# DMA transposes for q and the spatial weights, natural token order and a new order of units in an attention and gated-MLP kernel

## The chip, the cores and the metric

One core of a Trainium2 chip runs the whole program. The metric is device time in microseconds (us). *Slow* is a run more than 1.5% above the fastest of the same kernel; only fast runs are compared. Ratios are the mean time of one kernel's fast runs over the mean of the other's fast runs of the same rounds on the same chip, so not quite the ratio of the medians quoted beside them. A profile's span is about 1.8 us shorter than the time of the same run.

## The reference, cut to what matters

Four batches, eight heads, 768 tokens, head size 64. Each head's keys and values are mixed over 8 blocks of 96 tokens by a Sinkhorn-normalised 8x8 matrix P; attention runs inside each block; its output, 512 wide, goes through an MLP whose gate mixes tokens with a 768x768 matrix.

```python
k_sorted = np.einsum('bhij,bhjcd->bhicd', P, k_b)          # v the same
attn = softmax(scale * q_b @ k_sb^T)                       # inside a block of 96
x = (attn @ v_sb), heads side by side                      # 4 x 768 x 512
h = np.maximum(x @ w_in, 0.0); u, v = halves of h          # 512 wide each
v_n = (v - mean) / sqrt(var + 1e-6)
v_s = np.einsum('ts,bsd->btd', w_spatial, v_n) + b_spatial[None, :, None]
out = (u * v_s) @ w_out
```

## The kernel before

TensorE (PE), VectorE (DVE), ScalarE (ACT) and GpSimd (POOL) run a fixed list of units in program order, each written as letter, number, batch, copying engine and PSUM slot: `v`, `k` mix values and keys, `q` transposes q, `s` scores, `a` attend, `d` divide, `V`, `U` projections, `N` normalisation, `S` spatial product, `O` output projection. Batch b's MLP is interleaved with batch b+1's attention. There are four PSUM slots. In the tables and traces, xt is the divided attention output, lns the log-sum and then its exponential, vs the spatial sum, gt the gate product.

```python
# q: 48 transposes of 128x64 per batch on PE, two copies out of PSUM
nc.tensor.transpose(t[hh*64:hh*64+64, x, g*128:(g+1)*128],
                    q_in[self.b][:, 2*hp+hh, g*D:(g+1)*D], ident_bf)
copy(eng, qT, t[:, :, 0:S])
# spatial weights: 36 transposes of 128x128 on PE, six copies
nc.tensor.transpose(tp[:, 0, go*128:(go+1)*128],
                    wsp_nat[:, go, :].rearrange("p (s g) -> p g s", g=G)[:, gs, :], ident_bf)
# division: tokens stay in the order (g, block, t)
nc.scalar.activation(out=lns, in_=t[:, 1, 0:HW], func=AF.Ln)
nc.scalar.activation(out=lns, in_=lns, func=AF.Exp, scale=-1.0)
nc.vector.tensor_mul(
    out=self.xt[hp].rearrange("p (g i t) -> p i g t", g=G, i=NB)[:, i0:i0+NB//2],
    in0=t[:, 0, 0:HW].rearrange("p (i g t) -> p i g t", g=G, t=TB),
    in1=lns.rearrange("p (i g t) -> p i g t", g=G, t=TB))
# loads of batch b+2, issued by POOL before the first gate product of batch b
if not gmlp[b].gt and b + 2 < B:
    ... gate = two copies out of vb of batch b+1      # waits until vb has landed
    v_in[b+2], q_in[b+2], k_in[b+2] = load_heads(...), load_heads(...), load_heads(...)
    # [cut]
```

Loads are issued by POOL; stores, the trip of the mixed values through DRAM (`vd`, `vb`) and, in the changed kernel, the transposes are issued by the sync engine in order.

The softmax here doesn't subtract the row's maximum and nothing guards it: scores larger than these inputs give would overflow.

## Time and profile before

| | before |
|---|---|
| time, median of fast runs | 166.2 us |
| first projection (V00) starts, in the profile | 28.96 us |
| V00 to V01, V01 to V02, V02 to V03 | 37.9, 37.8, 33.7 us |
| V03 to the end | 29.4 us |

The rows below "first projection" are read from PE's timeline: V01 is the start of the first projection of batch 1, and so on; V00 is counted from where its matmuls run on (one single matmul of it stands earlier, at 28.13 us). The profile of before is of a slow run (169.51 us), so its stage times are up to 3.3 us long in sum.

### The profile page before, as it was taken

The numbers are of one execution on the slowest core, as the hardware profiler recorded it, in microseconds if no ns is written. First come the engines' busy times: TensorE is split into PE (matmuls) and PEld (weight loads), VectorE is DVE, ScalarE is ACT, GpSimd is POOL, SyncE is SP. The second block draws the span as 40 slices with busy tenths as digits, with TensorE's granted clock in tenths as the row PEclk, the third lists the DMA queues.
The fourth block names the chain that finished last, engine by engine and source line by source line (L and its number), as shares of the span: only waits on it lengthen the run. The fifth ranks groups of instructions, "written<-read, shape, count | busy, mean of one in ns | idle before, by whom it ended". The sixth has DMA issues, their size and how long they took to land.

```text
span 167.7 us, 3907 instructions
## 1 busy us (share of the span) xinstructions
PE 151.9 (91%) x1636; PEld 88.6 (53%) x1645; DVE 97.4 (58%) x203; ACT 110.0 (66%) x181; POOL 43.1 (26%) x46
## 2 busy tenths in 40 slices
PE   0989986999999999999994999999999999999780
PEld 0266853556855544457662454457665544556330
DVE  4667887158971562389222265789232658849951
ACT  3167997459877777689954586489959974560041
POOL 7931000970029550000049330000063300000000
PEclk9999997599999999999999699999999999999999
DMA  2999999999647997604329993605400036000045
GB/s 15 197 204 209 232 257 187 205 203 236 217 110 96 203 204 193 250 33 151 129 72 160 204 195 131 250 31 178 151 23 0 4 131 250 0 0 4 0 182 193
DMA packets 21554, 23.86 MB, mean 142 GB/s; under 512 B 736, under 2 KB 18144, under 8 KB 21408
## 3 DMA queue, kind: packets, MB, share of 16 engines
q0 software_dynamic: 13760, 12.58, 46.8%
q1 hardware_dynamic: 7776, 11.02, 18.3%
q8 instruction: 13, 0.21, 0.5%
q14 instruction: 5, 0.04, 0.1%
HBM read 27.14 MB, written 8.65 MB: 213 GB/s over the span
## 4 chain that ended last, share of the span: by engine, by line
PE 62%; DVE 11%; ACT 10%; DMA 6%; issue 6%; POOL 2%; DVEq 0%; POOLq 0%; SPq 0%; ACTq 0%
PE ps L393 13%; PE ps L443 13%; PE ps L465 10%; PE ps L428 9%; PE ps L352 4%; ACT ex L338 3%; DVE vs L454 3%; PE ps L331 3%; DMA vb<-vd 3%; PE ps L359 2%; DVE gt L455 2%; PE ps L288 2%; PE ps L246 2%; PE ps L276 2%; PE ps L212 2%
## 5 line engine op out<-in xcount | busy, mean ns | idle before, releaser
L443 PE MATMUL ps<-wspT,v_sb 128*128 128x384 bf16 x192 | 34.6, 334 | 0.0
L338 ACT ACTIVATE ex<-ps 96x768 bf16<-96x768 f32 x32 | 24.3, 806 | 8.4 <-PE ps L331 8.3
L454 DVE TENSOR_TENSOR vs<-ps,b_bc 128x768 f32<-128x768 f32 (+1 forms) x20 | 15.9, 794 | 23.7 <-PE ps L443 18.8
L375 DVE TENSOR_TENSOR xt<-ps,lns 128x384 bf16<-128x384 f32 x32 | 16.9, 554 | 19.9 <-ACT lns L371 19.9
L455 POOL TENSOR_TENSOR gt<-vs,u_sb 128x768 bf16<-128x768 f32 x12 | 19.7, 1651 | 34.1 <-ACT ex L338 31.3
L443 PEld LDWEIGHTS <-v_sb 128*128 128x128 bf16 x192 | 18.2, 100 | 12.6 <-issue 1.6
L393 PE MATMUL ps<-w_in_sb,xt 128*128 128x512 bf16 x94 | 24.1, 406 | 0.3 <-DVE xt L375 0.2
L465 PE MATMUL ps<-w_out_sb,gt 128*128 128x512 bf16 x90 | 21.9, 380 | 1.1 <-DVE gt L455 0.8
L407 DVE BATCH_NORM_STATS2 stats<-v_sb 128x6 f32<-128x512 bf16 x24 | 16.3, 677 | 11.0 <-ACT v_sb L227 10.9
L428 PE MATMUL ps<-xt,w_in_sb 128*128 128x384 bf16 x128 | 22.6, 326 | 0.0
L227 ACT ACTIVATE v_sb<-ps 128x1024 bf16<-128x1024 f32 (+1 forms) x15 | 12.5, 852 | 15.5 <-PE ps L393 15.5
L365 ACT ACTIVATE lns<-ps 128x384 f32<-128x384 f32 x32 | 14.5, 486 | 3.9 <-PE ps L359 3.8
L428 PEld LDWEIGHTS <-w_in_sb 128*128 128x128 bf16 x128 | 12.2, 98 | 8.1
L221 ACT COPY o_sb<-ps 128x256 f32<-128x256 f32 (+1 forms) x11 | 7.3, 663 | 13.8 <-DVE o_sb L223 12.1
L393 PEld LDWEIGHTS <-xt 128*128 128x128 bf16 x96 | 9.9, 104 | 12.1 <-issue 2.1
L371 ACT ACTIVATE lns<-lns 128x384 f32<-128x384 f32 x32 | 15.7, 525 | 0.2
L465 PEld LDWEIGHTS <-gt 128*128 128x128 bf16 x96 | 8.6, 98 | 12.4 <-DVE gt L455 1.3
L352 PE MATMUL ps<-ex,vb 96*64 96x96 bf16 x256 | 11.4, 210 | 3.4 <-DVE vs L454 2.5
L352 PEld LDWEIGHTS <-vb 96*64 96x64 bf16 x256 | 8.7, 109 | 8.5 <-issue 7.1
L227 ACT ACTIVATE u_sb<-ps 128x768 bf16<-128x768 f32 x13 | 10.3, 808 | 1.7 <-PE ps L428 1.2
L359 PE MATMUL ps<-ex,ones 96*64 96x384 bf16 x64 | 11.1, 332 | 0.0
L221 ACT CAST kT<-ps 128x768 bf16<-128x768 f32 x13 | 10.0, 806 | 1.1 <-PE ps L288 1.1
(73 smaller groups left out, 177.8 us busy)
## 6 DMA issues: line engine op xcount, KB each, us to landing
out_dram<-o_sb SPq DMA_DIRECT2D x9, 512.0 KB, 2.8
q_in<-in_q_dram POOLq DMA_DIRECT2D x4, 768.0 KB, 10.4
k_in<-in_k_dram POOLq DMA_DIRECT2D x4, 768.0 KB, 13.4
v_in<-in_v_dram POOLq DMA_DIRECT2D x4, 768.0 KB, 9.7
vd<-vm SPq DMA_DIRECT2D x6, 384.0 KB, 3.7
vb<-vd SPq DMA_DIRECT2D x6, 384.0 KB, 3.9
out_dram<-o_sb SPq DMA_DIRECT2D x6, 256.0 KB, 2.1
wsp_nat<-in_moe_w_spatial_dram POOLq DMA_DIRECT2D x1, 1152.0 KB, 21.9
```

The lines of the kernel that those rows point to most:

```text
L221: nc.scalar.copy(out=out, in_=in_)
L227: nc.scalar.activation(out=out, in_=in_, func=AF.Relu)
L338: nc.scalar.activation(out=e.rearrange("p h i c -> p h (i c)"), in_=t[0:BLK, :, 0:NB // 2 * BLK], func=AF.Exp, scale=scale,)
L352: nc.tensor.matmul(t[hh * 64:hh * 64 + 64, 0, ii * BLK:(ii + 1) * BLK], lhsT=self.vb[:, i, h // (H // 2), h % (H // 2), :], rhs=self.e[n][ ...
L375: nc.vector.tensor_mul(out=self.xt[hp].rearrange("p (g i t) -> p i g t", g=G, i=NB)[:, i0:i0 + NB // 2], in0=t[:, 0, 0:HW].rearrange("p (i ...
L393: nc.tensor.matmul(t[:, x, :], lhsT=self.xt[kc][:, g * 128:(g + 1) * 128], rhs=w_in_sb[:, kc, DH:DFF], start=(kc == 0), stop=(kc == KC - 1),)
L407: nc.vector.bn_stats(out=stats, in_=v_sb[:, x, :])
L428: nc.tensor.matmul(t[:, x, 0:HW], lhsT=w_in_sb[:, kc, mc * 128:(mc + 1) * 128], rhs=self.xt[kc][:, x * HW:(x + 1) * HW], start=(kc == 0), ...
L443: nc.tensor.matmul(t[:, x, 0:HW], lhsT=self.v[g][:, mc * 128:(mc + 1) * 128], rhs=wspT[:, g, x * HW:(x + 1) * HW], start=(g == 0), stop=(g ...
L454: nc.vector.tensor_add(out=vs[:, x], in0=t[:, x, 0:HW], in1=b2[:, x])
L455: eng.tensor_mul(out=gt2[:, x], in0=vs[:, x], in1=u2[:, x])
L465: nc.tensor.matmul(t[:, x, :], lhsT=self.gt[mc][:, g * 128:(g + 1) * 128], rhs=w_out_sb[:, mc, :], start=(mc == 0), stop=(mc == FC - 1),)
```

## The change

Its intent: TensorE is the busy engine, so take the transposes off it. q of batches 1 to 3 and the spatial weights go through transposing DMAs from SBUF to SBUF. For that, tokens must be in natural order, which the division produces by reading at a stride. The spreading of P moves to the start, idle matmuls are put into batch 0's attention to hold the clock, the loads move, and the units are reordered. Cut to its core:

```diff
+        def qdma(self, n, eng, ps):
+            qr = qr_pool.tile([128, G, H, D], BF16, name="qr", tag="qr")
+            nc.vector.tensor_copy(out=qr.rearrange("p g h d -> p h g d"), in_=q_in[self.b]...)
+            nc.sync.dma_start(out=self.q_tile(), in_=qr..., transpose=True)
+    def wsp_t():                       # called before the list of units
+        for g in range(G):
+            nc.sync.dma_start(out=wspT[:, :, g*128:(g+1)*128], in_=wsp_nat[:, g, :], transpose=True)
             # divide
-                out=self.xt[hp].rearrange("p (g i t) -> p i g t", ...)[:, i0:i0 + NB // 2],
-                in1=lns.rearrange("p (i g t) -> p i g t", g=G, t=TB),
+                out=self.xt[hp][:, ih*HW:(ih+1)*HW].rearrange("p (i t g) -> p i t g", ...),
+                in1=lns.rearrange("p (i g t) -> p i t g", g=G, t=TB),
             # first loads, in order
-        w_in, b, w_spatial, v1, k1, q1, w_out
+        w_in, v1, q1, w_spatial, k1, b, w_out
             # loads of batch b+2
-                    if not gmlp[b].gt and b + 2 < B:          # before gate product 1: v, q, k
+                    if len(gmlp[b].gt) == 2:                  # after gate product 2: gate, v
+                    elif len(gmlp[b].gt) == 4:                # after gate product 4: q, k
-                    eng = DVE if b == B - 1 else nc.gpsimd
+                    eng = DVE if b == B - 1 and len(gmlp[b].gt) == FC - 1 else nc.gpsimd
-        vs_pool bufs=2
+        vs_pool bufs=3
 ... [cut: pdiag straight from PSUM, two DVE block transposes of P, four idle matmuls
          in each attend unit of batch 0, natural rows in the store, the new list of units]
```

More of the change, by code (lines that the diff above doesn't have):

```diff
@@ L65 @@
     qk_pool = ctx.enter_context(tc.tile_pool(name="qk", bufs=7))
-    ex_pool = ctx.enter_context(tc.tile_pool(name="ex", bufs=7))
+    qr_pool = ctx.enter_context(tc.tile_pool(name="qr", bufs=1))
+    qt_pool = ctx.enter_context(tc.tile_pool(name="qt", bufs=2))
+    ex_pool = ctx.enter_context(tc.tile_pool(name="ex", bufs=8))
     xt_pool = ctx.enter_context(tc.tile_pool(name="xt", bufs=8))
-    ln_pool = ctx.enter_context(tc.tile_pool(name="ln", bufs=4))
+    ln_pool = ctx.enter_context(tc.tile_pool(name="ln", bufs=3))
     moe_pool = ctx.enter_context(tc.tile_pool(name="moe", bufs=4))
-    vs_pool = ctx.enter_context(tc.tile_pool(name="vs", bufs=2))
+    vs_pool = ctx.enter_context(tc.tile_pool(name="vs", bufs=3))
     vsb_pool = ctx.enter_context(tc.tile_pool(name="vsb", bufs=4))
@@ L88 @@
     nc.sync.dma_start(out=p_all, in_=sort_net.rearrange("b h i j -> (b h) i j"))
-    b_nat = pers.tile([128, S], FP32)
     def load_heads(x, b, name):
@@ L112 @@
     )
-    sel16 = const.tile([8, 128], BF16)
-    nc.gpsimd.memset(sel16, 0.0)
+    sel = const.tile([BH, NB // 2, 128], BF16)
+    nc.gpsimd.memset(sel, 0.0)
     nc.gpsimd.affine_select(
-        out=sel16.rearrange("p (j t) -> p j t", t=TB),
-        in_=sel16.rearrange("p (j t) -> p j t", t=TB),
-        pattern=[[1, NB], [0, TB]], compare_op=ALU.not_equal,
+        out=sel.rearrange("p i (j t) -> p i j t", t=TB),
+        in_=sel.rearrange("p i (j t) -> p i j t", t=TB),
+        pattern=[[NB, NB // 2], [1, NB], [0, TB]], compare_op=ALU.not_equal,
         fill=1.0, base=0, channel_multiplier=-1,
@@ L130 @@
     nc.gpsimd.dma_start(out=w_in_sb, in_=moe_w_in.rearrange("(kc p) f -> p kc f", p=128))
-    nc.gpsimd.dma_start(out=b_nat, in_=_raw_ap(moe_b_spatial, 0, [[0, 128], [1, S]]))
+    v_in[1] = load_heads(v, 1, "v_in")
+    q_in[1] = load_heads(q, 1, "q_in")
     wsp_nat = pers.tile([128, G, S], BF16)
-    nc.gpsimd.dma_start(out=wsp_nat, in_=moe_w_spatial.rearrange("(p g) s -> p g s", g=G))
-    v_in[1] = load_heads(v, 1, "v_in")
+    nc.gpsimd.dma_start(out=wsp_nat, in_=moe_w_spatial.rearrange("(g p) s -> p g s", p=128))
     k_in[1] = load_heads(k, 1, "k_in")
-    q_in[1] = load_heads(q, 1, "q_in")
+    b_bc = pers.tile([128, S], FP32)
+    nc.gpsimd.dma_start(out=b_bc, in_=_raw_ap(moe_b_spatial, 0, [[0, 128], [1, S]]))
     w_out_sb = pers.tile([128, FC, DM], BF16)
@@ L172, with make_pdiag, transpose_p @@
     prep_sb = pers.tile([128, B, NB, H], BF16)
-    pts = {}
-    def spread_t(b, nb, ps):
-        n = nb * NB * H
-        t = ps_tile(ps)
-        for i in range(NB):
-            nc.tensor.matmul(
-                t[0:NB, 0, 0:n].rearrange("p (b i h) -> p b i h", i=NB, h=H)[:, :, i, :],
-                lhsT=p_bf[:, i, :], rhs=ident_bf[0:BH, b * H:(b + nb) * H],
-                start=True, stop=True,
-            )
-        pts[b] = small.tile([NB, B * NB * H], BF16, name="pt", tag="pt", bufs=2)
-        nc.vector.tensor_copy(out=pts[b][:, 0:n], in_=t[0:NB, 0, 0:n])
+    pdiag = [pd_pool.tile([128, H, NB, TB], BF16, name="pdiag") for _ in range(B)]
+    def make_pdiag(b, eng, h0, n, src=None):
+        base = h0 if src is not None else b * NB * H + h0
+        src = prep_sb if src is None else src
+        eng.tensor_mul(
+            out=pdiag[b][:, h0:h0 + n],
+            in0=_raw_ap(mask16, 0, [mask16.ap[0], [0, n], [TB, NB], [1, TB]]),
+            in1=_raw_ap(src, base, [src.ap[0], [1, n], [H, NB], [0, TB]]),
+        )
+    p_t = pers.tile([BH, 2, BH], BF16)
+    def transpose_p():
+        for x in range(2):
+            nc.vector.transpose(
+                out=p_t[:, x, :], in_=p_bf[:, x * (NB // 2):(x + 1) * (NB // 2), :].rearrange("p i j -> p (i j)"),
+            )
     def spread(b, nb, ps):
@@ L191, in spread @@
         t = ps_tile(ps)
-        nc.tensor.matmul(t[:, 0, 0:n], lhsT=sel16, rhs=pts[b][:, 0:n], start=True, stop=True)
-        nc.vector.tensor_copy(
-            out=prep_sb[:, b:b + nb].rearrange("p b i h -> p (b i h)"), in_=t[:, 0, 0:n],
-        )
-    pdiag = [pd_pool.tile([128, H, NB, TB], BF16, name="pdiag") for _ in range(B)]
-    def make_pdiag(b, eng, h0, n):
-        eng.tensor_mul(
-            out=pdiag[b][:, h0:h0 + n],
-            in0=_raw_ap(mask16, 0, [mask16.ap[0], [0, n], [TB, NB], [1, TB]]),
-            in1=_raw_ap(prep_sb, b * NB * H + h0, [prep_sb.ap[0], [1, n], [H, NB], [0, TB]]),
-        )
-    b_bc = pers.tile([128, S], FP32)
-    wspT = pers.tile([128, G, S], BF16)
-    def wsp_unit(gs, eng, ps):
-        tp = ps_tile(ps, BF16)
-        for go in range(G):
-            nc.tensor.transpose(
-                tp[:, 0, go * 128:(go + 1) * 128],
-                wsp_nat[:, go, :].rearrange("p (s g) -> p g s", g=G)[:, gs, :],
-                ident_bf,
+        if b:
+            nc.tensor.matmul(t[:, 1, :], lhsT=ident_bf, rhs=warm_sb, start=True, stop=True)
+        for i in range(NB):
+            nc.tensor.matmul(
+                t[:, 0, 0:n].rearrange("p (b i h) -> p b i h", i=NB, h=H)[:, :, i, :],
+                lhsT=sel[:, i % (NB // 2), :],
+                rhs=p_t[:, i // (NB // 2), b * H:(b + nb) * H],
+                start=True, stop=True,
+            )
+        if b == 0:
+            for h0, nh in ((0, 2), (2, 2), (4, 4)):
+                make_pdiag(0, DVE, h0, nh, t.rearrange("p x c -> p (x c)"))
+        else:
+            nc.vector.tensor_copy(
+                out=prep_sb[:, b:b + nb].rearrange("p b i h -> p (b i h)"), in_=t[:, 0, 0:n],
+            )
+    wspT = pers.tile([128, G, S], BF16)
+    def wsp_t():
+        for g in range(G):
+            nc.sync.dma_start(
+                out=wspT[:, :, g * 128:(g + 1) * 128], in_=wsp_nat[:, g, :], transpose=True,
             )
-        copy(eng, wspT[:, gs, :], tp[:, 0, 0:S])
     def copy(eng, out, in_):
@@ L238, in __init__ @@
             self.vm = None
-            self.q, self.k, self.e, self.vT = {}, {}, {}, {}
+            self.qT, self.q, self.k, self.e, self.vT = None, None, {}, {}, {}
             self.xt, self.vb, self.acc, self.mixed = {}, None, {}, []
@@ L267, in vmix, with q_tile @@
                 )
+        def q_tile(self):
+            if self.qT is None:
+                self.qT = qt_pool.tile([128, G * H // 2, 128], BF16, name="qT", tag="qT")
+                self.q = self.qT.rearrange("p (g h) (i t) -> p h i g t", g=G, i=NB)
+            return self.qT
         def qtr(self, n, eng, ps):
             t = ps_tile(ps, BF16)
-            qT = qk_pool.tile([128, 2, S], BF16, name="qT", tag="q", bufs=3)
             for x in range(2):
-                hp = 2 * n + x
                 for g in range(G):
@@ L277, in qtr @@
                             t[hh * 64:hh * 64 + 64, x, g * 128:(g + 1) * 128],
-                            q_in[self.b][:, 2 * hp + hh, g * D:(g + 1) * D],
+                            q_in[self.b][:, 2 * (2 * n + x) + hh, g * D:(g + 1) * D],
                             ident_bf,
                         )
-                self.q[hp] = qT[:, x, :].rearrange("p (g i t) -> p i g t", g=G, i=NB)
-            copy(eng, qT, t[:, :, 0:S])
+            copy(
+                eng,
+                self.q_tile().rearrange("p (g h) c -> p h g c", g=G)[:, 2 * n:2 * n + 2],
+                t[:, :, 0:S].rearrange("p x (g c) -> p x g c", g=G),
+            )
+        def qdma(self, n, eng, ps):
+            qr = qr_pool.tile([128, G, H, D], BF16, name="qr", tag="qr")
+            nc.vector.tensor_copy(
+                out=qr.rearrange("p g h d -> p h g d"),
+                in_=q_in[self.b].rearrange("p h (g d) -> p h g d", g=G),
+            )
+            nc.sync.dma_start(
+                out=self.q_tile(), in_=qr.rearrange("p g h d -> p (g h d)"), transpose=True,
+            )
         def mixed_t(self, src, hp, eng, ps):
@@ L333, in score @@
                         lhsT=self.k[hp][rows, i * BLK:(i + 1) * BLK],
-                        rhs=self.q[hp][rows, i],
+                        rhs=self.q[rows, hp, i],
                         start=True, stop=True,
@@ L348, in attend @@
             t = ps_tile(ps)
+            if self.b == 0:
+                for _ in range(2):
+                    for hh in range(2):
+                        nc.tensor.matmul(
+                            t[hh * 64:hh * 64 + 64, 1, HW:512], lhsT=ones,
+                            rhs=warm_sb[0:BLK, 0:512 - HW], start=True, stop=True,
+                        )
             for ii in range(NB // 2):
@@ L373, in divide @@
                 self.xt[hp] = xts[self.b, hp] = xt_pool.tile([128, S], BF16, name="xt", tag="xt")
-            i0 = ih * (NB // 2)
             nc.vector.tensor_mul(
-                out=self.xt[hp].rearrange("p (g i t) -> p i g t", g=G, i=NB)[:, i0:i0 + NB // 2],
-                in0=t[:, 0, 0:HW].rearrange("p (i g t) -> p i g t", g=G, t=TB),
-                in1=lns.rearrange("p (i g t) -> p i g t", g=G, t=TB),
+                out=self.xt[hp][:, ih * HW:(ih + 1) * HW].rearrange(
+                    "p (i t g) -> p i t g", t=TB, g=G,
+                ),
+                in0=t[:, 0, 0:HW].rearrange("p (i g t) -> p i t g", g=G, t=TB),
+                in1=lns.rearrange("p (i g t) -> p i t g", g=G, t=TB),
             )
@@ L439, in spatial @@
             pairs = [(g, x) for g in range(G) for x in range(2)]
-            if self.last:
+            final = self.last and len(self.gt) == FC - 1
+            if final:
                 pairs = [(g, x) for x in range(2) for g in range(G)]
@@ L452, in spatial @@
             )
-            for x in (slice(0, 1), slice(1, 2)) if self.last else (slice(0, 2),):
+            for x in (slice(0, 1), slice(1, 2)) if final else (slice(0, 2),):
                 nc.vector.tensor_add(out=vs[:, x], in0=t[:, x, 0:HW], in1=b2[:, x])
@@ L470, in oproj @@
             o_sb = o_pool.tile([128, 2, DM], FP32, name="o_sb", tag="o")
-            o_dram = out[self.b].rearrange("(p g) n -> p g n", g=G)[:, 2 * n:2 * n + 2, :]
+            o_dram = out[self.b].rearrange("(g p) n -> p g n", p=128)[:, 2 * n:2 * n + 2, :]
             if self.last:
@@ L482 @@
     SCHEDULE = """
-        k00A0 k30A1 k20D2 s00-3 k10D0 s70-1 s50-2 t30D3 t10A0 t00D1 s20-2 s60-3 B30D0 s10-1
-        B10D2 s30-3 t20D0 a70-1 s40-2 B00D3 d70-- a20-0 B20D2 d20-- a00-3 a10-1 d00-- a40-2
-        d10-- d40-- a30-0 a50-3 d30-- a60-1 P00-2 d50-- d60-- R00-0 V00-2 w50A3 w30A1 V10-0
-        w40D2 v11A3 V20-1 v01A0 U00D3 v21A2 v31A1 U10A0 w20D2 w10D1 w00A3 k11D0 k21A2 q01D1
-        k01A3 q11D0 k31D2 N00-- s31-1 U20A3 s11-0 s21-1 S00-2 s61-3 s41-0 U30A1 s51-2 s01-3
-        S10-0 a01-1 d01-- a41-2 d41-- S20-3 a11-0 a51-1 d51-- d11-- S30-2 s71-3 a21-1 a61-0
@@ L489 @@
-        a31-2 d61-- d31-- O20A3 a71-0 d21-- O10A2 d71-- O00A3 V01-1 V21-2 v02A0 V11-3 v12A1
-        U01A2 U11D0 N01-- v22A3 v32A1 U21A2 k12A0 q12D3 k02A1 q02A2 k22A0 k32A3 S01-1 s42-2
-        s02-0 S11-3 s72-1 s52-2 S21-0 s32-3 s22-1 U31A2 a42-0 a02-3 d42-- d02-- s12-1 S31-2
-        s62-0 a32-3 a72-1 d32-- a12-2 d72-- d12-- O21A0 a52-3 d52-- a22-1 a62-2 d22-- d62--
-        O01D0 O11D3 V02-1 V22-2 v03A0 V12-3 v13A1 U02A2 U12D0 N02-- v23A3 v33A1 U22A2 k13A0
-        q13D3 k03A1 q03A2 k23A0 k33A3 S02-1 s43-2 s03-0 S12-3 s73-1 s53-2 S22-0 s33-3 s23-1
@@ L495 @@
-        U32A2 a43-0 a03-3 d43-- d03-- s13-1 S32-2 s63-0 a33-3 a73-1 d33-- a13-2 d73-- d13--
-        O22A0 a53-3 d53-- a23-1 a63-2 d23-- d63-- O02D0 O12D3 V03-1 V13-2 V23-0 N03-- U03A3
-        U13A1 U23A2 U33A0 S03-3 S13-1 S23-2 S33-0 O03A3 O13A1 O23A2
+        k00A2 k10A3 k20D0 s10-1 k30D2 s20-3 s40-0 s50-1 t10D2 s70-3 t30D0 s60-1 B10D2 s00-3
+        t00D0 s30-1 B30D2 a20-3 t20D0 d20-- a60-1 B00D2 d60-- a30-0 d30-- B20D3 a10-2 a00-1
+        d10-- d00-- a70-0 a50-3 d70-- a40-2 d50-- d40-- q01A- v21A1 v01A0 V00-3 V10-2 V20-1
@@ new lines @@
+        v11A0 U20A3 N00-- U10A2 U30A1 U00D0 k11A3 k01D2 k21A1 v31D0 s21-3 s31-2 k31D1 s51-0
+        s41-3 s11-2 s61-1 S10-0 s01-3 s71-2 S20-1 a31-0 a11-3 d11-- a01-2 S00-1 d31-- d01--
+        S30-3 a61-1 a41-0 a71-2 d71-- d61-- d41-- O00A3 a21-2 a51-1 d21-- d51-- O20D0 O10D3
+        V01-2 v22A1 q02A- v02A0 V11-3 V21-2 v12A1 v32A0 U11A3 k02D2 N01-- k32A1 U31A0 k12D3
+        k22A2 S11-1 s42-0 s62-2 U21D3 s02-1 s22-0 S21-2 s72-3 s12-1 U01A0 a22-2 d22-- a12-3
+        d12-- s32-1 S01-0 S31-2 s52-3 a02-1 a42-0 d42-- d02-- a32-2 O11D3 a52-0 d32-- d52--
@@ L498 @@
+        O01D1 a72-3 a62-2 d72-- d62-- O21A0 V02-1 v23A3 q03A- v03A2 V12-0 V22-1 v13A3 v33A2
+        U12A0 k03D1 N02-- k33A3 U32A2 k13D0 k23A1 S12-3 s43-2 s63-1 U22D0 s03-3 s23-2 S22-1
+        s73-0 s13-3 U02A2 a23-1 d23-- a13-0 d13-- s33-3 S02-2 S32-1 s53-0 a03-3 a43-2 d43--
+        d03-- a33-1 O12D0 a53-2 d33-- d53-- O02D3 a73-0 a63-1 d73-- d63-- O22A2 V03-3 V13-0
+        V23-1 N03-- U03A2 U13A3 U23A0 U33A1 S03-2 S13-3 S23-0 S33-1 O03A2 O13A3 O23A0
     """
     UNITS = {
-        "v": "vmix", "k": "ktr", "q": "qtr", "s": "score", "a": "attend", "d": "divide",
+        "v": "vmix", "k": "ktr", "q": "qdma", "s": "score", "a": "attend", "d": "divide",
@@ L509 @@
         attn[0].qtr(0, ACT, 2), attn[0].qtr(1, ACT, 3)
-        spread_t(0, 1, 0), warm(1, 1)
-        spread(0, 1, 0)
-        make_pdiag(0, DVE, 0, 2), make_pdiag(0, DVE, 2, 6)
-        warm(4, 1)
+        warm(2, 1)
+        transpose_p()
+        spread(0, 1, 0), spread(1, 3, 1)
+        for x in range(1, B):
+            make_pdiag(x, nc.gpsimd, 0, H)
+        wsp_t()
         for step in SCHEDULE.split():
@@ L517 @@
             ps = None if step[4] == "-" else int(step[4])
-            if name == "P":
-                spread_t(1, 3, ps)
-            elif name == "R":
-                spread(1, 3, ps)
-                for x in range(1, B):
-                    make_pdiag(x, nc.gpsimd, 0, H)
-                nc.gpsimd.tensor_copy(
-                    out=b_bc.rearrange("p (g c) -> p g c", g=G),
-                    in_=b_nat.rearrange("p (c g) -> p g c", g=G),
-                )
-            elif name == "w":
-                wsp_unit(n, eng, ps)
-            elif name in "VNUSO":
+            if name in "VNUSO":
                 if b not in gmlp:
@@ L533 @@
                 if name == "S":
-                    if not gmlp[b].gt and b + 2 < B:
+                    eng = DVE if b == B - 1 and len(gmlp[b].gt) == FC - 1 else nc.gpsimd
+                getattr(gmlp[b], UNITS[name])(n, eng, ps)
+                if name == "S" and b + 2 < B:
+                    if len(gmlp[b].gt) == 2:
                         gate = small.tile([1, 2], BF16, name="gate", tag="gate")
@@ L540 @@
                         v_in[b + 2] = load_heads(v, b + 2, "v_in")
+                    elif len(gmlp[b].gt) == 4:
                         q_in[b + 2] = load_heads(q, b + 2, "q_in")
                         k_in[b + 2] = load_heads(k, b + 2, "k_in")
-                    eng = DVE if b == B - 1 else nc.gpsimd
-                getattr(gmlp[b], UNITS[name])(n, eng, ps)
             else:
```

## The prediction

> **What bounds the kernel now.** I read the page's slices first, then the chain of work that ended last in order of time, then the timelines of PE, DVE, ACT and POOL, and the windows view where the clock dipped.
>
> The page's head and slices (busy tenths; PEclk is the granted TensorE clock):
>
> ```profile
> PE 151.9 (91%) x1636; PEld 88.6 (53%) x1645; DVE 97.4 (58%) x203; ACT 110.0 (66%) x181; POOL 43.1 (26%) x46
> ...
> PE   0989986999999999999994999999999999999780
> ...
> PEclk9999997599999999999999699999999999999999
> DMA  2999999999647997604329993605400036000045
> ```
>
> From 29 us to 157 us TensorE is busy in nearly every slice, with one hole near 85 to 92 us. Each slice is 4.2 us. DMA is full for the first 40 us. The chain agrees: in batches 0 to 3 it is a list of matmul groups that follow each other end to end, so there a matmul taken away is time taken away:
>
> ```profile
> 41.32 1.00 PE ps L212 x18
> 42.32 0.79 PE ps L288 x24
> 43.11 0.67 PE ps L276 x24
> 43.78 0.34 PE ps L288 x12
> 44.12 0.67 PE ps L276 x24
> 44.79 0.34 PE ps L288 x12
> ```
>
> L276 is the transpose of q, L212 that of the spatial weights. On the chain 24 q transposes take 0.67 us, 28 ns each (two halves of the array at once); the 219 ns per instruction in the groups view is latency, not pace. The 18 weight transposes take 1.00 us, 56 ns each.
>
> Three places are not bound by the pace of the matmuls. (1) 13 to 29 us, attention of batch 0: ACT is busy 15.06 of 16 us between 12 and 28. (2) Just after it the clock is halved (columns: length; busy and count of PE, PEld, DVE, ACT, POOL; PEclk; DMA; GB/s):
>
> ```profile
> 26.00:28.00 2.00, 0.95 (x19) 0.61 (x18) 1.44 (x4) 2.00 (x6) 0.00 (x0) 0.83 1.02 181
> 28.00:30.00 2.00, 1.78 (x5) 0.73 (x6) 1.07 (x3) 0.16 (x1) 0.84 (x1) 0.50 1.31 209
> 30.00:32.00 2.00, 2.00 (x10) 0.93 (x8) 0.00 (x0) 0.24 (x1) 2.00 (x2) 0.50 1.30 195
> ```
>
> (3) The hole at 89 us: POOL waited, in order, for the second half of vb, then issued three loads, and only then did the first gate product of batch 1 run; DVE's third sum waited for its vs buffer, and PE for the PSUM that this sum was to free:
>
> ```profile
> DVE vs L454 <- POOL gt L455: 4.8, 1, 4.8
> ...
> PE ps L352 <- DVE vs L454: 2.5, 1, 2.5
> ```
>
> The profile is a slow run (169.51 us against a timed median of 166.38), so some of such stalls, 3.1 us in all, is not in the number to be beaten.
>
> **What the Trainium skill says.** "DMA: Bandwidth & Descriptors", section "Latency and other measured facts", gives a transposing DMA an effective 261 GB/s when its middle dimension is not contiguous; "VectorE: DVE Perf Modes", section "The three transpose paths", gives 1309 ns for one 128x128 block. The kernel before has no transposing DMA, so no run here shows it yet. "TensorE: Matmul & The Clock Gate", section "HAM oscillation — how this bites in real kernels", warns of half clock after gaps over about 3.4 us; here the clock halved after a stretch where PE was busy 1.23 and 0.95 of 2 us, with no gap above 1.03 us, so the trace shows that a thin stretch is enough. "Advanced Engine Details and Errata", section "SBUF Cachelines", says that touching a different 16-byte line with each access costs: the row sum over 64 contiguous fp32 takes 207 ns and the column sum with a 32-byte stride 253 ns, so the trace agrees, with some 0.7 ns per element.
>
> **The change part by part**, in what it does to the end:
>
> a) Start. p_bf is ready at 11.22 us, and the first k matmul runs at 13.27: PE transposes, a copy, the spreading matmul, a copy, the first pdiag. New: two DVE block transposes (I estimate 0.2 us each from the 0.21 us of 32x64 operations), eight matmuls (0.34 us), pdiag of two heads straight from PSUM (0.42 us as now) and handoffs, 1.3 us. Saves 0.7 us.
>
> b) Attention of batch 0, ACT-bound. One kT copy goes from ACT to DVE (0.80 us), and the spreading of batches 1 to 3, which puts 0.25 us of DVE on the chain and 1.03 us of PE idleness just before the first projection, moves to the start. Against this, DVE was busy 12.45 of 16 us there and gets one more copy (0.95), the prep copy (0.35) and divisions that read lns at a 64-byte stride: by the 0.7 ns above at most 0.27 us each, 2.1 us for eight. That makes about 15.9 us, as full as ACT. I count 0.5 us saved.
>
> c) Batch 0's projections to batch 1's scores. 36 weight transposes gone: 36 x 56 ns = 2.0 us. 48 q transposes gone: 48 x 28 ns = 1.3 us. The halved clock cost 2.77 - 6 x 0.216, plus 1.28 - 12 x 0.056, plus 2.35 - 8 x 0.216 = 2.7 us. The change puts four zero matmuls of 128 columns into each of eight attend units: 32 x 28 ns = 0.9 us of PE work in a stretch that waits for ACT anyway, meant to hold the clock. It lifts PE from about half busy to perhaps 65%; I give it half of the 2.7: 1.35 us. Together 4.7 us.
>
> d) Batches 2 and 3: 2 x 48 x 28 ns = 2.7 us, all on the chain. The 0.96 us DVE copies and 1.44 us ACT copies of q that go, and the three SBUF copies of 128x3072 that come (about 0.9 us each by the 0.41 us of a 512-element bf16 pass, at least that pace), are beside PE work.
>
> e) The hole at 89 us: loads of v now go out after the second gate product and q, k after the fourth, and vs has three buffers. In the profile it costs 2.5 us of PE idleness and 1.1 us of slow clock (12 spatial matmuls in 3.18 against 2.06 us), but the timed runs have 3.1 us less than the profile. I count 0.5.
>
> f) Tail. In the last batch each spatial product now costs DVE 0.96 us of sum, with the product on POOL (1.64), except the last one. Before, DVE did 0.55 + 0.56 twice per unit, 2.2 us against PE's 2.0, and fell behind: PE ended at 156.5, DVE at 159.76, and the output projection waited 0.81 us. New: DVE trails PE by about 1.1 us, its last first half ends near 157.0 and the output matmuls run through, 24 x 0.216 us after 156.5, ending at 161.8 instead of 162.7. Saves 1.0 to 1.4; I take 1.2.
>
> Sum: 0.7 + 0.5 + 4.7 + 2.7 + 0.5 + 1.2 = 10.3 us.
>
> New cost: the DMA transposes must land in time. Loads landed in order, 3.9 us apart per head tensor and 5.5 for the weights; in the new order q of batch 1 is there at about 29.5, the weights at 35, k of batch 1 at 39 us. Six weight transposes of 192 KB and one q transpose of 768 KB are 1.97 MB, at the skill's 261 GB/s an estimated 7.5 us plus about 2 us of latency, and they share full DMA engines with k and w_out. PE, by its own work, reaches the first k unit of batch 1 at about 39 and the first spatial unit at about 42 us; the transposes may end at 42 to 45. I count 1 us of PE waiting, possibly 4. In later batches the q transpose starts some 12 us of PE work ahead of its first score, with 5 us or so to do: hidden. Natural token order costs PE nothing (projections read the same 128-column slices), and 2 KB rows of output instead of 4 KB nothing that the end sees.
>
> 166.4 - 10.3 + 1.0 = 157.1; as the stalls that I did not count can only shrink with later loads, I say **156.5 us**.
>
> **Rivals.** First: the transposes take the place of the work removed, as a wait. For it: DMA share is full until 40 us, the sync queue runs in order, so vd and vb stand behind 5 us of q transposes, and vb already took 11.5 us from the first store to the last landing. Against: 12 us of slack per batch. If each transpose took 15 us rather than 5, scores would wait some 4 us per batch, with a halved clock after: 166 to 170 us. Second: DVE becomes the bound through the strided divisions, 32 x 0.27 = 8.6 us more. For it: section (b). Against: in batches 2 and 3 DVE is busy under 20 of 34 us, and k copies that read PSUM at a stride already run at 953 ns for 768, no slower than contiguous ones (1215 for 1024). It would cost 1 to 2 us in batch 0 only: 158. Third: everything works and the clock never drops: the full 2.7 of (c), the full stall of (e), no waits: 152.
>
> **Range and chances.** The PE work removed (c and d without clock, 6.0 us, plus a and f, 1.9 us) is read from the chain and nearly sure: alone it gives 158.5. The clock and the stall can add 4, waits can take 1 to 6. So 152 to 161.5 for 8 in 10. Within 2% means 163.05 or more: it needs over 6 us of new waiting. Chances: faster 0.87, same 0.09, slower 0.04.
>
> **What would show it.** Right: PE loses about 5 us of transposes (180 instructions); PE follows itself without gaps in batches 2 and 3; 32 to 32.5 us from one batch's first projection to the next (33.7 before between batches 2 and 3); clock at 0.9 or more in every slice after the start; nothing waits for wspT or qT; the division still near 0.55 us. Wrong: PE waiting for a DMA that writes qT, wspT or vb; a division of 0.8 us with DVE full in batch 0; the clock still at half near 28 us; POOL late with the gate product.

## The result, and the profile after

The changed kernel takes **181.56 us** (180.41 to 182.67, 4 runs) against 166.22: ratio 1.092, 95% interval 1.085 to 1.099. It is 9% slower; I had said 6% faster.

The slices of the changed kernel's page (busy tenths of 4.5 us each):

```profile
PE   1869995996029998992799999994999999999990
...
PEclk9996999999557999999699999998799999999999
DMA  3999999999985359999980197999570006200035
```

Where PE had one hole, it has three, near 42 to 52, 81 to 86 and 121 to 123 us, and the granted clock dips in or after each. The page's chain that ended last, shares by engine, then by line:

```profile
PE 36%; DMA 36%; POOL 8%; SPq 6%; DVE 5%; ACT 3%; issue 3%; POOLq 1%; DVEq 0%; ACTq 0%
DMA k_in<-in_k_dram 18%; DMA wsp_nat<-in_moe_w_spatial_dram 15%; PE ps L475 14%; PE ps L459 9%; SPq L220 6%; PE ps L497 4%; PE ps L354 3%; DMA qT<-qr 3%; POOL gt L487 3%; DVE vs L486 3%; PE ps L311 3%; PE ps L424 3%; DVE xt L404 2%; POOL q_in L93 2%; ACT lns L395 1%
```

PE's share fell (it was 62%) and DMA's rose to 36% (it was 6%): transfers became the path. PE's timeline has the waits in brackets (columns: start, length, engine, line, operation, tiles, count):

```profile
42.64 0.50 PE L251 MATMUL ps<-v_in,pdiag 128*128 128x384 bf16 x2
52.33 0.88 PE L354 MATMUL ps<-qT,kT 64*96 64x96 bf16 x16 [9.19 <-DMA qT<-qr]
...
85.96 1.20 PE L311 MATMUL ps<-pdiag,k_in 128*64 128x128 bf16 x24 [4.57 <-DMA k_in<-in_k_dram]
87.09 2.74 PE L459 MATMUL ps<-xt,w_in_sb 128*128 128x384 bf16 x8
...
123.10 0.86 PE L311 MATMUL ps<-pdiag,k_in 128*64 128x128 bf16 x24 [2.32 <-DMA k_in<-in_k_dram]
123.89 2.74 PE L459 MATMUL ps<-xt,w_in_sb 128*128 128x384 bf16 x8
```

9.19 us for the transposed q of batch 1; 4.57 and 2.32 us for k of batches 2 and 3. After each of the last two, eight projection matmuls take 2.74 us instead of 1.46: the clock is halved (the windows view has 0.55 from 86 to 89 us, 0.62 from 123.2 to 126). The chain has k of batch 2 from issue to landing (columns: start, length, engine, tiles):

```profile
69.35 16.56 DMA k_in<-in_k_dram
```

Why q is late is in the sync queue's timeline:

```profile
35.30 11.25 SPq L220 DMA_TRANSPOSE wspT<-wsp_nat  x6
46.59 3.71 SPq L303 DMA_TRANSPOSE qT<-qr  x1
```

The six weight transposes stand first, cannot start before the weights land at 35.3, and hold the queue for 11.25 us; q, copied and ready at 31.9, is issued at 46.6. And the division, from the groups of the page, before and then after (last number before the second bar: mean ns):

```profile
L375 DVE TENSOR_TENSOR xt<-ps,lns 128x384 bf16<-128x384 f32 x32 | 16.9, 554 | 19.9 <-ACT lns L371 19.9
```

```profile
L404 DVE TENSOR_TENSOR xt<-ps,lns 128x384 bf16<-128x384 f32 x32 | 24.6, 803 | 12.8 <-ACT lns L401 12.5
```

It grew from 554 to 803 ns, as (b) of the prediction feared. In sum:

| stage | before (slow run) | after | best version (e6) |
|---|---|---|---|
| start to V00 | 29.0 | 31.1 | 28.9 |
| V00 to V01 | 37.9 | 42.3 | 37.3 |
| V01 to V02 | 37.8 | 39.1 | 34.0 |
| V02 to V03 | 33.7 | 37.1 | 32.6 |
| V03 to end | 29.4 | 28.9 | 28.6 |

### The profile page after: what moved, and what is told of

Same layout as the page of the kernel before. It is cut to its first block, busy times and chain, and to the rows that moved or that the text cites. A ratio compares the mean times of both kernels' runs of the same rounds, so it can differ in the third digit from the quotient of the medians.

```text
span 178.6 us, 3606 instructions
## 1 busy us (share of the span) xinstructions
PE 147.5 (83%) x1484; PEld 83.5 (47%) x1493; DVE 106.4 (60%) x198; ACT 99.8 (56%) x168; POOL 47.0 (26%) x48
## 4 chain that ended last, share of the span: by engine, by line
PE 36%; DMA 36%; POOL 8%; SPq 6%; DVE 5%; ACT 3%; issue 3%; POOLq 1%; DVEq 0%; ACTq 0%
DMA k_in<-in_k_dram 18%; DMA wsp_nat<-in_moe_w_spatial_dram 15%; PE ps L475 14%; PE ps L459 9%; SPq L220 6%; PE ps L497 4%; PE ps L354 3%; DMA qT<-qr 3%; POOL gt L487 3%; DVE vs L486 3%; PE ps L311 3%; PE ps L424 3%; DVE xt L404 2%; POOL q_in L93 2%; ACT lns L395 1%
## 5 line engine op out<-in xcount | busy, mean ns | idle before, releaser
L487 POOL TENSOR_TENSOR gt<-vs,u_sb 128x768 bf16<-128x768 f32 x15 | 24.6, 1640 | 118.6 <-ACT ex L361 84.6
L475 PE MATMUL ps<-wspT,v_sb 128*128 128x384 bf16 x192 | 32.9, 327 | 0.0
L404 DVE TENSOR_TENSOR xt<-ps,lns 128x384 bf16<-128x384 f32 x32 | 24.6, 803 | 12.8 <-ACT lns L401 12.5
L459 PE MATMUL ps<-xt,w_in_sb 128*128 128x384 bf16 x128 | 25.0, 351 | 0.0
L228 DVE CAST kT<-ps 128x768 bf16<-128x768 f32 x12 | 11.4, 957 | 19.9 <-PE ps L311 19.8
L424 PE MATMUL ps<-w_in_sb,xt 128*128 128x512 bf16 x94 | 21.8, 379 | 0.9 <-DVE xt L404 0.6
L354 PE MATMUL ps<-qT,kT 64*96 64x96 bf16 x256 | 11.4, 234 | 9.3 <-DMA qT<-qr 9.2
L354 PEld LDWEIGHTS <-kT 64*96 64x96 bf16 x256 | 8.9, 143 | 13.8 <-issue 13.3
L311 PE MATMUL ps<-pdiag,k_in 128*64 128x128 bf16 x192 | 8.4, 245 | 6.9 <-DMA k_in<-in_k_dram 6.9
L226 ACT COPY o_sb<-ps 128x256 f32<-128x256 f32 (+1 forms) x9 | 5.3, 585 | 13.5 <-DVE o_sb L228 11.8
```

The costliest lines, as they stand in the source:

```text
L354: nc.tensor.matmul(t[0:BLK, hh, ii * BLK:(ii + 1) * BLK], lhsT=self.k[hp][rows, i * BLK:(i + 1) * BLK], rhs=self.q[rows, hp, i], start=Tru ...
L404: nc.vector.tensor_mul(out=self.xt[hp][:, ih * HW:(ih + 1) * HW].rearrange("p (i t g) -> p i t g", t=TB, g=G,), in0=t[:, 0, 0:HW].rearrang ...
L424: nc.tensor.matmul(t[:, x, :], lhsT=self.xt[kc][:, g * 128:(g + 1) * 128], rhs=w_in_sb[:, kc, DH:DFF], start=(kc == 0), stop=(kc == KC - 1),)
L459: nc.tensor.matmul(t[:, x, 0:HW], lhsT=w_in_sb[:, kc, mc * 128:(mc + 1) * 128], rhs=self.xt[kc][:, x * HW:(x + 1) * HW], start=(kc == 0), ...
L475: nc.tensor.matmul(t[:, x, 0:HW], lhsT=self.v[g][:, mc * 128:(mc + 1) * 128], rhs=wspT[:, g, x * HW:(x + 1) * HW], start=(g == 0), stop=(g ...
L487: eng.tensor_mul(out=gt2[:, x], in0=vs[:, x], in1=u2[:, x])
```

## The experiments

The theory after the result: two independent waits make the loss, qT of batch 1 (held up behind the weight transposes) and k of batches 2 and 3 (loaded too late), and the division adds to batch 0. Rivals: the DMA engines are simply full, so order does not matter; or DVE is the cause.

### e1: weights back on TensorE

```diff
-        wsp_t()
+        ... w00A3 w10D2 w20A1 w30D0 w40A3 w50D2 ...      # after U00; PE transposes of wsp_nat[:, go, gs*128:...]
```

> The changed kernel with one part undone: the spatial weights are transposed by TensorE again (36 transposes and 6 copies, in the schedule after batch 0's last u projection), q stays with DMA. Theory: the 9.2 us that PE waits at 43 us for qT of batch 1 come from the six weight transposes that stand before it on the sync queue (35.3 to 46.6 us, because they wait for the weights that land at 35 us). Then qT of batch 1 is issued right after its DVE copy, near 32 us, and lands by 42; the wait is gone, 2 us of PE work come back: 181.5 - 9.2 + 2.0 = 174 us. Rival 1: the DMA engines are full with loads until 40 us and the q transpose is as late anyway: over 179 us. Rival 2: it is the order of the loads (k of batch 1 last), then PE waits for k_in of batch 1 instead: some 178.

Measured: 180.59 us, ratio 1.088. My expectation of 174 failed and rival 1 came true. The sync queue of e1, then PE's timeline:

```profile
31.38 12.77 SPq L313 DMA_TRANSPOSE qT<-qr  x1
```

```profile
50.11 0.87 PE L364 MATMUL ps<-qT,kT 64*96 64x96 bf16 x16 [4.73 <-DMA qT<-qr]
```

q is issued at once, but one transpose that took 3.71 us in the changed kernel now takes 12.77 us to issue and 18.6 us to land (at about 50 us), beside full loads. PE still waits 4.73 us for it, and has 2.4 us more of its own work. So queue order was only part of it. (What made the transpose slow is argued here and tested in e8.)

### e2: q and k of batch b+2 loaded with v

```diff
-                    elif len(gmlp[b].gt) == 4:
                         q_in[b + 2] = load_heads(q, b + 2, "q_in")
```

> The changed kernel, but q and k of batch b+2 are loaded together with v after the second gate product instead of after the fourth. Theory: the waits of PE for k_in in batches 2 and 3 (4.6 and 2.3 us) and the halved clock after each (about 1.7 us each) come from loads issued 5.3 and 6.8 us later than they could be; both gone: 181.5 - 10 = 171 to 173 us. Rival 1: the loads land late because the q transposes, vd/vb and output stores share the DMA engines with them; then half of the wait stays: 176 or more. Rival 2: issuing two more loads ahead of the third gate product makes POOL late and PE waits there instead: about 179.

Measured: 171.93 us, ratio 1.036: the theory, to the number. Both waits for k are gone (PE's wait for k_in in batches 2 and 3 is 0.0, weight loads 0.3 us), and V01 to V02 takes 32.8 us instead of 39.1. POOL's issue of k of batch 2, and its first product on PE, are now:

```profile
66.28 0.89 POOL L93 DMA_DIRECT2D k_in<-in_k_dram  x1
```

```profile
83.16 0.86 PE L311 MATMUL ps<-pdiag,k_in 128*64 128x128 bf16 x24
```

The wait for qT of batch 1 stays at 7.5 us. Of the 15 us lost, about 10 were the place of two loads in POOL's program.

### e3: Ln permutes instead of the division

```diff
-            nc.scalar.activation(out=lns, in_=t[:, 1, 0:HW], func=AF.Ln)
+            nc.scalar.activation(out=lns as "p (i t g)", in_=t[:, 1, 0:HW] as "p (i g t) -> p i t g", func=AF.Ln)
-                in1=lns.rearrange("p (i g t) -> p i t g", g=G, t=TB),
+                in1=lns.rearrange("p (i t g) -> p i t g", t=TB, g=G),
```

> The changed kernel, but Ln reads PSUM in natural token order and writes lns contiguously, so that the division reads lns at unit stride; it still reads PSUM at a stride. Theory: the division grew from 554 to 803 ns because it reads SBUF at a 64-byte stride; then it falls to about 555 ns, Ln stays near 485, DVE leaves batch 0's attention earlier and the first projection starts about 1.5 us sooner; 179.5 to 180.5 in all, since the q wait of batch 1 behind it does not depend on PE and absorbs it. Rival: the stride in PSUM is what costs; then the division stays near 800 and nothing changes, and Ln grows too.

Measured: 181.83 us, ratio 1.093 (one of its four runs, 183.27, is slow): the time of the changed kernel, where I had expected 179.5 to 180.5. The tile view of lns (count: minimum, median, maximum ns):

```profile
L395 ACT ACTIVATE lns<-ps x32: 470/486/499, 21.3 to 149.9; 128x384 f32<-128x384 f32 x32
...
L407 DVE TENSOR_TENSOR xt<-ps,lns x32: 544/557/558, 22.5 to 151.3; 128x384 bf16<-128x384 f32 x32
```

The cause of the longer division is settled: in this kernel reading SBUF at a 64-byte stride costs 250 ns per 384 elements, reading PSUM at the same stride costs neither DVE nor ACT anything. V00 starts at 28.9 instead of 31.1, but not all of this is the division: the profile of the changed kernel has a dip of the clock between 13 and 18 us that e3's has not (see e12). Among profiles without the dip V00 starts at 29.8 (e1, e4) and 28.9 (e3, e6), so the division is worth 1.0 us; among those with it 31.1 (changed kernel) and 29.5 to 29.7 (e5, e11, e12), 1.4 to 1.6. PE then waits 11.8 us for qT instead of 9.2: the gain is taken by the wait that does not depend on PE.

### e4: e1 and e2 together

```diff
-        wsp_t()
+        ... w00A3 w10D2 w20A1 w30D0 w40A3 w50D2 ...
-                    elif len(gmlp[b].gt) == 4:
```

> e1 and e2 together. Theory: the two waits are independent and add: 181.5 - 7 - 9.5 = 164 to 166 us, about as fast as the kernel before. Rival: removing the first wait brings the later loads no earlier relative to PE, so part of the gain is lost to the second: 168 or more.

Measured: 169.93 us, ratio 1.025, where I had expected 164 to 166: the number of the rival (168 or more). Less than the sum that I had expected, since e1 alone gives little; 3.82 us of waiting for qT of batch 1 are left. V01 to V02 takes 34.4 us, with 1.44 of waiting before the k product, and V02 to V03 33.1. The clock is also at 0.52 to 0.63 from 30 to 34 us, in batch 0's projections, where e6's is at 1.00: the idle matmuls before them do not hold it in every profile.

### e5: e4 and e3 together

```diff
+                out=lns.rearrange("p (i t g) -> p i t g", t=TB, g=G),      # of Ln, on top of e4
-                in1=lns.rearrange("p (i g t) -> p i t g", g=G, t=TB),
+                in1=lns.rearrange("p (i t g) -> p i t g", t=TB, g=G),
```

> e4 (weights on TensorE, loads early) with Ln permuting as in e3. In e3 the division fell from 803 to 557 ns and PE began the projections 2 us sooner, but the wait for qT behind them grew by the same amount. Theory: with most waits gone the shorter division shows: one batch takes 32.4 instead of 33.1 us in batches 2 and 3, and 0 to 2 us come off batch 0; 169.9 - 2 = 167 to 168.5 us. Rival: the gaps of PE between attend units come from ACT (Ln and Exp), then a batch still takes 33.1 us and the time stays within 0.5 of 169.9.

Measured: 169.19 us, ratio 1.019 (1.011 to 1.027; e4's is 1.017 to 1.033, so the two are not apart beyond noise; one of e5's four runs is slow, 171.24). I had expected 167 to 168.5. The mechanism shows in the trace (V02 to V03 takes 32.6 instead of 33.1 us); the total gains less, because the wait for qT grew to 4.78 us and took the gain of batch 0 again.

### e8: the loads beside the q transpose taken away

```diff
-    nc.gpsimd.dma_start(out=wsp_nat, ...)       # and k of batch 1, b_bc, w_out_sb
+        for y in (k_in[1], wsp_nat, b_bc, w_out_sb):
+            nc.gpsimd.memset(y, 0.0)
```

> Wrong result on purpose, to measure the disputed cost by itself: e1, but the four loads that follow q of batch 1 (weights, k of batch 1, bias, output weights) are replaced by zeros written by POOL, so the DMA engines are idle when q of batch 1 is transposed. Theory: the transpose of q at 31 us took 12.8 us to issue and 18.6 us to land in e1 because 16 full engines are shared with the loads; alone it takes 3.7 us to issue and about 5.6 to land, as at 46 us in the changed kernel, and PE does not wait for qT. Rival: a transpose from SBUF to SBUF is slow near 31 us for another reason (the descriptors, or the DVE copy before it): over 10 us again.

Measured (wrong result on purpose, one run, state unknown, 173.21 us), the sync queue, then PE:

```profile
31.32 3.67 SPq L310 DMA_TRANSPOSE qT<-qr  x1
```

```profile
45.25 0.73 PE L361 MATMUL ps<-qT,kT 64*96 64x96 bf16 x16
```

The same instruction at the same time: 3.67 us to issue and about 5.6 to land instead of 12.77 and 18.6, and PE does not wait for it. So this transpose is over three times slower beside full loads. This is also why e1 failed. (The waits for k of batches 2 and 3 remain in e8, 4.06 and 3.40 us: it has the late loads.) The Trainium skill says in "DMA: Bandwidth & Descriptors", section "Queues, rings and completion order", that each engine takes turns between the queues it has work for, a packet at a time; the slowing agrees with that, though no run here shows the turns themselves.

### e6: q of batch 1 on TensorE as well, only batches 2 and 3 by DMA

```diff
-        ... q01A- v21A1 ...  U30A1 U00D0 w00A3 w10D2 w20A1 w30D0 w40A3 w50D2 k11A3 ...
+        ... v21A1 ...  U30A1 U00D0 q01A3 q11D2 w00A1 w10D0 w20A3 w30D2 w40A1 w50D0 k11A3 ...   # on top of e5
```

> e5 with q of batch 1 transposed by TensorE too; only q of batches 2 and 3 by DMA. Theory: what is left of the wait at 47 to 51 us in e4 (3.8 us, plus 1.5 us of halved clock after it) is the q transpose slowed by full DMA queues; it goes, and 1.3 us of PE work comes back: 162.5 to 165, faster than the kernel before. Rival: k_in of batch 1, which landed near 39 to 41 us, becomes the wait; then 166 or more.

Measured: **163.38 us** (163.06 to 163.58), ratio 0.986, interval 0.979 to 0.993: faster than both kernels, than the one before by 1.4% (the interval lies wholly below 1, but not below 0.98, so the 2% verdict is "unclear"). The copies of the weight transposes also change PSUM slots and engines. Its slices:

```profile
PE   0949997999999979996999999999999999999980
...
PEclk9999999999999999999999999999999999999999
```

The wait at 43 to 52 us is gone and the clock does not drop in this profile. Two waits are left: 1.32 us for k of batch 2 and 1.09 us for a gate product on POOL.

### e9: no DMA transposes at all

```diff
-        V01-2 v22A1 q02A- ...        k22A2 S11-1 ...                          # on top of e6; batch 3 likewise
+        V01-2 v22A1 ...              k22A2 q02D1 q12A0 S11-1 ...
-                unit = "qtr" if name == "q" and b in (1,) else UNITS[name]
+                unit = "qtr" if name == "q" and b in (1, 2, 3) else UNITS[name]
```

> e6 with q of batches 2 and 3 on TensorE as well: no DMA transposes at all, but the new order of units, natural token order with the permuting Ln, the early loads, the new tail. Theory: where the DMA transposes are hidden (batches 2 and 3) they are worth the 1.3 us of PE per batch that I predicted, so this is 2.5 to 3 us slower than e6. Rival: the q transposes on the sync queue delay vd, vb and the stores and give that back; then this is as fast as e6 or faster.

Measured: 168.04 us, ratio 1.015, 4.7 us slower than e6; I had expected 2.5 to 3. (Three of its four runs, 167.85 to 168.13, have a clock of 0.998 or more; the profiled one, 169.06, has the dip at 13 to 18 us.) PE's timeline of e9 shows why:

```profile
114.13 1.51 PE L296 MATMUL ps<-ident_bf,q_in 128*64 128x128 bf16 x48
116.79 2.11 PE L488 MATMUL ps<-wspT,v_sb 128*128 128x384 bf16 x12 [1.16 <-DVE qT L238]
```

Beside the 1.3 us of transposes comes 1.16 us of waiting for the copy out of PSUM (0.85 us in batch 2), in the place where I put the units; V01 to V02 takes 36.4 us against 34.0, V02 to V03 35.2 against 32.6. So in batches 2 and 3, where they are hidden, the DMA transposes are worth what PE work and copies cost: the intent of the change holds there. How much of the copy's wait a better place would save is open.

### e7: e6 with the weights by DMA

```diff
+        wsp_t()
-        ... U00D0 q01A3 q11D2 w00A1 w10D0 w20A3 w30D2 w40A1 w50D0 k11A3 ...
+        ... U00D0 q01A3 q11D2 k11A3 ...
```

> e6 but with the spatial weights transposed by DMA as in the change (q of batch 1 stays on TensorE). Theory: the six weight transposes can start only when the weights land, near 35 us, and with full DMA engines take about 11 us to issue, so wspT is complete near 49 to 51 us; e6 needs it at 47.8 and, with 2.5 us of TensorE transposes gone, would need it at about 45.3: PE waits 4 to 6 us, maybe with a halved clock, 2 to 4 us slower than e6: 165 to 167. Rival: the transposes run beside the loads without slowing, done by 44; then 2 us faster than e6: 161.5.

Measured: 167.42 us, ratio 1.010, 4 us slower than e6. The theory had 2 to 4 us (165 to 167) with 4 to 6 us of waiting; the waits came smaller, and other terms made the sum. PE waits 0.56 and then 1.99 us in the middle of its first spatial unit, and the rest of it runs at a lower clock (11 matmuls take 3.63 us, where 12 take 2.12 in e6); later a gate product is late by 2.6 us (1.1 in e6):

```profile
49.14 3.63 PE L478 MATMUL ps<-wspT,v_sb 128*128 128x384 bf16 x11 [1.99 <-DMA wspT<-wsp_nat]
...
64.16 2.20 PE L500 MATMUL ps<-w_out_sb,gt 128*128 128x512 bf16 x7 [2.61 <-POOL gt L490]
```

### e10 and e11: other orders of the loads on top of e6

e10 loads v, k, q; e11 loads v and k after the second gate product and q after the fourth.

```diff
-                        q_in[b + 2] = load_heads(q, b + 2, "q_in")
                         k_in[b + 2] = load_heads(k, b + 2, "k_in")
+                    elif len(gmlp[b].gt) == 4:                             # e11 only
+                        q_in[b + 2] = load_heads(q, b + 2, "q_in")
```

> e6 with k loaded before q in batches 2 and 3 (v, k, q instead of v, q, k). e6 still waits 1.3 us for k of batch 2, whose load ran beside the q transpose. Theory: k then lands before the q transpose starts, and q still lands before its copy at 70.8 us: 1.3 us faster, 162. Rival: q lands later, the q transpose starts later and PE waits for qT instead: 163.4 or more.

> e6 with v and k loaded after the second gate product and q after the fourth. Theory: besides the k wait (1.3 us) this takes 0.9 us of issue work from ahead of POOL's third and fourth gate products, for which the output projection of batch 0 waits 1.09 us in e6: 161.5. Rival: q of batch 2 lands only after 72 us, its transpose ends after 80 us and the scores wait: 164 or more.

Measured: e11 169.6 us, ratio 1.023, so its rival won, in number. e10's four runs: 166.06 to 170.25; its one fast run, 166.06, is not the 162 expected. Its profile is of a slow run, so I read the mechanism from e11 alone. It is not the one that I had named. DVE's timeline of e11, then PE's:

```profile
70.47 0.18 DVE L452 BATCH_NORM_AGGREGATE mv<-stats 128x2 f32<-128x6 f32 x1
76.08 0.96 DVE L309 COPY qr<-q_in 128x3072 bf16<-128x3072 bf16 x1 [5.43 <-DMA q_in<-in_q_dram]
```

```profile
81.14 0.85 PE L321 MATMUL ps<-pdiag,k_in 128*64 128x128 bf16 x12 [4.57 <-DVE kT L238]
```

The scores do not wait for qT. The copy that prepares the transpose stands in DVE's fixed order, so when q is late all of DVE waits 5.43 us, then PE 4.57 for a copy of k that stands behind it.

e10 rested on k of batch 2 being late because its load ran beside the q transpose. The trace of e9, where no transpose runs, speaks against that: the weights of the same k product are just as late there (PE's weight loads wait for the load of k 1.81 us in e9, 1.71 in e6). In e11, with k issued before q, they do not wait for it.

### e12: the fourth gate product on DVE

```diff
-                    eng = DVE if b == B - 1 and len(gmlp[b].gt) == FC - 1 else nc.gpsimd
+                    eng = DVE if len(gmlp[b].gt) == FC - 1 else nc.gpsimd
```

> e6 with the fourth gate product of each batch on DVE (0.95 us) instead of POOL (1.64). In e6 the output projection of batch 0 waits 1.09 us for POOL's last product, because POOL issues three loads (2.7 us) between the second and the third. Theory: that wait goes and nothing else moves: 162.3, 2.2 to 2.5% faster than the kernel before. Rival: the extra 0.95 us on DVE delays the divisions that the same output projections' PSUM waits for: 163.4 or more.

Measured: 164.44 us, ratio 0.990 (0.986 to 0.994; 0.979 to 0.993 for e6): no gain. The wait for POOL is still 1.11 us, since it is for the third product, which I had not looked at closely enough. V00 also starts 0.85 us later (29.70) with a lower clock around 15 us, and the wait for k is 1.70 us. That dip of the clock between 13 and 18 us comes and goes between profiles that are alike up to there (the changed kernel, e2, e5 and e8 to e12 have it, with a mean clock of about 0.66 in these 5 us; e1, e3, e4, e6 and e7 have 1.00); what sets it is open, and with it about 1 us of any difference here.

## Why the prediction was wrong

**The step that failed is the last one, "New cost", and with it the sentence "the stalls that I did not count can only shrink with later loads".** I put 1 us, "possibly 4", for all new waiting. The profile shows 16.1 us of PE waiting for transfers (9.2 + 4.6 + 2.3) and, by the groups right behind each wait against the same groups elsewhere, an estimated 4.5 us of halved clock. With the late loads mended (e2) 9.6 us come back, and with q of batch 1 off the DMA engines as well (e6, which has also the weights on TensorE and the Ln change) the kernel takes 163.38.

- *k of batches 2 and 3*: 6.9 us of waiting that I did not list, not even among the rivals. I looked at later loads only as something that frees POOL. In the profile the loads of q and k of batch 2 are issued at 68.4 and 69.4 us and k lands at 85.9, where the new list of units wants it at 81.4. e2 shows that this and its clock are worth 10 us.
- *Transposes in batch 1*: I estimated 7.5 + 2 us for 1.97 MB from the skill's 261 GB/s; from 35.3 to 52.3 us it took 17. e8 and e1 show it for q: 5.6 us in quiet, 18.6 beside full loads. In the changed kernel it is the weights' transposes that run beside loads (11.25 us to issue six), and q behind them takes 3.71; that loads slow the weights' transposes in the same way is by analogy, no run has them in quiet. I had written that the engines are full and still used the rate of a transfer alone. The first rival named this form of loss, but saw it in every batch; in batches 2 and 3 qT is never waited for.
- *(a) Start*: 0.7 us predicted, nothing came: the first k matmul is at 13.19 us (13.21 in PE's timeline before). The path from p_bf is shorter by some 0.5 us, but p_bf is ready at 11.69 instead of 11.22, because one Sinkhorn product on DVE takes 0.68 instead of 0.21 us beside a POOL selection that grew (below).
- *(b) Batch 0*: 0.5 us saved was predicted; V00 starts 2.2 us later. The working was right in its size (0.27 us more per division at most; 0.25 measured) and in naming DVE as full; the conclusion "as full as ACT", hence harmless, was the error. The profiles of e1, e3, e4 and e6 put the division at 1.0 us, those with the dip of the clock at 1.4 to 1.6; the rest of the 2.2 goes with the dip, whose cause is open.
- *(c), (d) PE work removed*: right. V02 to V03 takes 33.1 us with the division of the change (e4), and 32.6 with Ln permuting (e5, e6), against the predicted "32 to 32.5". The DMA transposes of batches 2 and 3 are hidden, as predicted, though not at the predicted length: they took 7.28 and 5.39 us to issue and about 9 to land, and were hidden because the first scores came 11 to 13.6 us after their issue. e9 puts their worth above my number, with 0.85 and 1.16 us of waiting for copies in it that depend on the place of the units.
- *(e)*: the hole at 89 us is gone, and the late k came in its place.
- *(f) Tail*: 1.0 to 1.4 predicted; from the last batch's first spatial matmul to the end it is 18.3 us after 160.34, against 19.0 after 148.69: 0.75. The chain of waits of the changed kernel ends through POOL's third product and the last 20 output matmuls, which I had passed over.

## What to carry to other kernels

Moving work from a busy engine to DMA pays where the transfer, slowed by what runs beside it, still lands before its first use: here it does in batches 2 and 3, where it has 11 us or more, and does not in the first 50 us, when loads fill the DMA engines. A rate measured in quiet must not be used for a transfer beside full loads. When loads are moved to free an engine, work out for each its landing against its first use, since the list of units moves both; and remember that a preparatory copy in an engine's fixed order makes that whole engine wait for its load. A step that makes PE arrive earlier at a wait that does not depend on PE gains nothing until that wait is gone (e3), so remove the waits first and judge the rest after.

## What the Trainium skill lacked or had wrong

- "DMA: Bandwidth & Descriptors" (section "Latency and other measured facts") gives a transposing DMA two bandwidths, 261 GB/s with a non-contiguous middle dimension and about 350 to 400 contiguous, and says nothing of other traffic beside it. One SBUF-to-SBUF transpose of 128x3072 bf16 took 3.67 us to issue and 5.6 to land in quiet (e8), 12.77 and 18.6 beside full loads (e1).
- The same page, section "Issuing engines are not separate DMA queues", calls the time on the sequencer usually small beside the DMA itself. For these transposes it is most of it: 3.7 of 5.6 us in e8; a transfer of vb holds the sync queue 0.32 us.
- "Advanced Engine Details and Errata", section "SBUF Cachelines", names no size of the penalty. A DVE product whose fp32 operand in SBUF is read at a 64-byte stride took 803 ns for 384 elements, at unit stride 557; the same stride in PSUM cost nothing for DVE, and for ACT 486 ns as before (e3). The section "PSUM Cachelines" there speaks of matmuls only.
- "TensorE: Matmul & The Clock Gate", section "HAM oscillation — how this bites in real kernels", ties the half clock to gaps over about 3.4 us. It also came after a wait of 2.32 us (eight matmuls in 2.74 instead of 1.46 us), and between 13 and 18 us in some profiles, with no gap over 1.75 us before it once PE had begun. The page's next section tells of short idle times that bring it too, but gives no length.
- An agreement, not a lack: "SBUF — State Buffer", section "Terms", says that DVE and GpSimd lock a shared port pair and that the loser blocks for the whole instruction. The changed kernel fits that: a 32x64 product of DVE that takes 0.21 us elsewhere ends at 6.42 us, just after POOL's selection at 6.37. No run here separates the two. POOL's line, then DVE's:

```profile
5.50 0.87 POOL L115 TENSOR_SCALAR_AFFINE_SELECT sel<-sel 32x512 bf16<-32x512 bf16 x1
```

```profile
5.74 0.68 DVE L163 TENSOR_TENSOR p_all<-p_all,colsum 32x64 f32<-32x64 f32 x1
...
7.96 0.21 DVE L163 TENSOR_TENSOR p_all<-p_all,colsum 32x64 f32<-32x64 f32 x1
```
